# Three orders rewritten in a fused attention and SiLU kernel: v's loads ahead of the reciprocals' copies, x's sums ahead of the additions, one couple's q ahead of its k

## The chip, the cores and the metric

One core of a Trainium2 chip runs the whole kernel. Its engines are TensorE (PE, with weight loads shown apart as PEld), VectorE (DVE), ScalarE (ACT), GpSimd (POOL) and SyncE (SP), which here only issues DMAs. Each engine works through its own instructions in the order in which the program lists them, and waits on semaphores for the others. The metric is the device time of one execution in microseconds (us), taken as the median of several executions.

## The reference

`q`, `k`, `v` are 8 batches x 12 heads x 448 positions x 64 dimensions, float32. The output of attention becomes the input x of a two-layer network with 3584 tokens, 768 -> 2048 -> 768:

```python
def rmsnorm(x, g):
    rms = np.sqrt(np.mean(x * x, axis=-1, keepdims=True) + 1e-06)
    return x / rms * g
q_n, k_n = rmsnorm(q, g_q), rmsnorm(k, g_k)
scores = np.matmul(q_n, k_n.transpose(0, 1, 3, 2)) / np.sqrt(64)
attn = np.exp(scores - scores.max(-1, keepdims=True))
attn = attn / (attn.sum(-1, keepdims=True) + 1e-09)
x = np.matmul(attn, v)           # then (B,H,S,D) -> (B*S, H*D)
h = x @ w_in
out = (h / (1 + np.exp(-h))) @ w_out
```

## The kernel before, in words

**Couples.** Attention is worked off in 24 couples of four heads each, c = 0 to 23; three couples make a batch, and GROUP = 6 couples make two batches. `visit(c)` holds scores, exponentials and weighted sums of couple c, mixed with the end of couple c - 1; `between(c)` holds what lies between two visits: the transposes of the next q and k, the sums of the exponentials and their reciprocals, the rounding of `w_in` and, from c = 6 on, a share of the first layer's matmuls for the two batches finished before. From c = 12 (LATE) on, q and k come in another layout.

**The order is written by hand.** The program runs under a manual schedule, so the order in which Python calls issue instructions is the order on each engine; only different engines may overtake each other. `fill(others, prompt)` deals such work out between the first layer's matmuls.

**A couple's path.** `scores` (L712) writes a PSUM tile `sc`, of which there are two, and ACT turns it into exponentials (L717). `weigh` (L749) multiplies them with v into the two PSUM banks `av0` and `av1`. A couple's banks are read out in the next visit: by a copy (L1412) for couples 0 to 4, by the division `divide` (L808) from couple 5 on. Only then may the next couple's first `weigh` write them. `turn` (L725) writes one column of a bank by ACT or DVE, before the last `weigh` of the couple before. The last scores of a couple (LEFT) are written by ACT over a tile that the first addition `add(c, 1)` (L763, DVE) reads, so that exponential waits for this addition.

**Reciprocals and their copies.** `sum_up` adds up the exponentials on PE with ones (L783), DVE takes reciprocals in two halves (L792), and `spread` copies them over the partitions by DMA: four copies (L799), then two (L801) that wait for the four. `divide` needs them. For couples 0 and 1 the first half's reciprocal runs in the next visit (1 and 2), and the second half with `spread` at that visit's end (`inverting.pop()()`, L1446). SP issues these copies.

**v.** `load_v` (L313) loads 256 KB into the only buffer for the first two thirds of a couple's keys; it waits for the last `weigh` that reads the buffer, `weigh(c, 1, 0)` at L1447. The remaining keys have buffers of their own (L326, L329).

**q and k of the next couple.** `normalise(c)` gives four pieces, q in two halves and k in two halves. Each squares a half on ACT (L467, into one of two scratch tiles, the first halves both into one, the second halves both into the other) and reduces it on DVE (L468); then comes a tiny DVE operation (L492), POOL takes the root (L496), and for q POOL multiplies q itself (L511, two instructions). PE transposes q in `transpose_q` (L629).

**The sums of x.** The first layer is one level of Strassen's scheme with seven products (L899 in `Seven.product`, two PSUM banks `mm` in this phase). Its right-hand sides are sums of quarters of x: `right_sums` makes four DVE subtractions (L854) for each of three column blocks, `sum_x(group, 0)`, `sum_x(group, 1)`, `sum_x(group, 2)`. Block 0 needs no x of the group's last couple, blocks 1 and 2 do. They run at c = 6, 12 and 18 for the two batches before. Results are taken from the banks by DVE (L857), or by ACT (L907, L917).

**Rounding of w_in** (only at early couples): ACT L100 and L101, DVE L123, L126, L130, POOL L134; `sum_w_in` adds sums of it on DVE (L854 and L857 of 128x768).

**Late couples' q**: `sum_squares` and `scale` (L684 on PE, L685 on DVE, L688 and L691 on POOL), then `flip` (L655 on DVE).

Of the kernel before, what the change touches and what calls it, by code (L numbers as in the profile page):

```python
# [535 lines left out]
def bounded(  # L536
# [4 lines left out]
    HW, HF = z.NW // 2, z.NF // 2  # L541
# [8 lines left out]
    GROUP, LATE = z.NPAIR, z.LATE  # L550
# [88 lines left out]
    def transpose_k(c):  # L639


        assert z.KB == BANK
        t = ps.tile([P, 2, BANK], F32, name="sc", bufs=2)
        rows = place[f"k{c % 2}"]
        for i in range(2):
            for j in range(z.KEYS + 1 - i):
                nc.tensor.transpose(t[:, i, ts(j, P)], rows[:, ds((z.KA, z.KB)[i] + j * P, P)], ident)
        columns = t.rearrange("p i s -> p (i s)")[:, 0 : z.NK]
        nc.scalar.activation(kT, columns, AF.Copy, scale=gains)
        loads["k" if c < LATE - 1 else "quarters"](min(c + 2, LATE))  # L650
# [71 lines left out]
    def turn(step, copy):  # L722

        if step != weighed["step"]:
            copy(banks[1][:, S : S + 1], minus_half)  # L725
# [86 lines left out]
    def normalise(c):  # L812


        def piece(name, i):
            t = scratch[i if c < GROUP + 2 else 0]
            source = raw_of(c) if c < GROUP else q_of(c)
            if name == "q":
                norm.squares_q(c, source, t, i)
            else:  # L820
                norm.squares_k(c, place["k0" if c >= LATE else f"k{c % 2}"], t, i)
            if name == "q" and c < GROUP:
                norm.root(c, name, i)
                norm.scale(c, source, q_of(c), i, nc.gpsimd)
                if i == 1 and c + 2 < GROUP:
                    load_q(c + 2)
            elif i == 1:
                norm.root(c, name)
                if name == "q":
                    for m in range(2):  # L830
                        norm.scale(c, source, q_of(c), m, nc.gpsimd)
                elif LATE <= c < NC - 1:
                    loads["k"](c + 1)

        if c >= NC:
            return []
        return [lambda a=a: piece(*a) for a in (("q", 0), ("q", 1), ("k", 0), ("k", 1))]
# [15 lines left out]
    def minus(a, b, out):  # L853
        nc.vector.tensor_tensor(out=out, in0=a, in1=b, op=ALU.subtract)  # L854
# [11 lines left out]
                lambda: minus(a12, s2, s4),  # L866
            )[step]()

    def right_sums(b11, b12, b21, b22, t1, t2, t4):

        minus(b12, b11, t1)
        minus(b22, t1, t2)
        minus(b22, b12, b12)
        minus(b21, t2, t4)

    ps_alone = None
    turns = dict(next=0)
# [66 lines left out]
    def fetch_ahead(group, m):  # L944
        rows = [staged(), extra_stage if m else staged()]
        nc.sync.dma_start(rows[0], ahead[m])
        return rows, part_in(group, m, rows)
# [15 lines left out]
    def quarters(group, c):  # L963

        return [xT(b, c + up) for up in (0, HW) for b in group]

    def sums_of_x(c):
        return [sums_x[:, ts(i * HW + c, S)] for i in range(3)]

    def sum_x(group, c):  # L970
        right_sums(*quarters(group, c), *sums_of_x(c))

    def part_in(group, m, rows, prompt=False):

# [404 lines left out]
    def weights_in(c, half):  # L1379
        i = 2 * (c - GROUP) + half  # L1380
        work = [step_of[step] for step in halves.get(i, "ro" if c < GROUP else "")]
        return work + [lambda a=a: sum_w_in(*a) for a in sums_halves.get(i, ())]
# [8 lines left out]
    def last_two(c):  # L1391
        return [c // GROUP * 2 - 2, c // GROUP * 2 - 1]

    def visit(c):

        beside = normalise(c + 1) if 0 < c < GROUP else []
        if c < NC:
            scores(c, 0, 0)
        if c == 0:
            normalise_alone(1)  # L1400
        run_all(beside[0:1])
        if c > 0:
            weigh(c - 1, LEFT)
            weigh(c - 1, LEFT - 1, 0)
            turn(1, nc.scalar.copy if c <= GROUP else nc.vector.tensor_copy)
        if c < NC:
            scores(c, 0, 1)
        if c > 0:
            weigh(c - 1, LEFT - 1, 1)
            if c - 1 < EARLY:  # L1410
                for i in range(2):
                    nc.vector.tensor_copy(x_of(c - 1, i), sums[i])  # L1412
                run_all(beside[1:2])
                if inverting:
                    if c > 1:
                        divide(c - 2, None)
                    while len(inverting) > (c < GROUP // 2):
                        inverting.pop(0)()
            else:
                divide(c - 1, sums)  # L1420
                run_all(beside[1:2])
                if c < NC and c % GROUP == 0:
                    sum_x(last_two(c), 0)
                weights_in_visit(c)
            if c + 1 < NC:
                loads["vrest"](c + 1)
        if c == NC:
            return
        scores(c, 1, 0)
        scores(c, 1, 1)  # L1430
        if c < GROUP:
            run_all(beside[2:3])
        weigh(c, 0, 1)
        scores(c, 2, 0)
        weigh(c, 1, 1)
        turn(0, nc.scalar.copy)
        if c < GROUP:
            run_all(beside[3:4])
        scores(c, 2, 1)
        weigh(c, 0, 0)  # L1440
        run_all(add(c, 1))
        if c >= GROUP and c % GROUP == 0:
            for i in range(1, HW):
                sum_x(last_two(c), i)
        if len(inverting) == 1:
            inverting.pop()()  # L1446
        weigh(c, 1, 0)  # L1447
        if c < GROUP // 2:
            room.w_in.open()
        scores(c, LEFT)  # L1450
        if c + 1 < NC:
            loads["v"](c + 1)

    def run_all(work):
        for piece in work:
            piece()

    def between(c):

        def transposes_and_sums():  # L1460
            summing = sum_up(c)
            if c < GROUP:
                next(summing)
            if c == GROUP - 1:
                reciprocals = next(summing)
                divide(c - 1, None)
                run_all(reciprocals)
                transpose_k(c + 1)
                return
            if c < LATE - 1:  # L1470
                transpose_k(c + 1)
            reciprocals = next(summing)
            if LATE - 1 <= c < NC - 1:
                reciprocals += [lambda: flip(c + 1, "k"), gain]
            if GROUP // 2 <= c < EARLY:
                divide(c - 1, None)
            return reciprocals

        if c < LATE - 1:
            transpose_q(c + 1)  # L1480
        elif c < NC - 1:
            flip(c + 1, "q")
        if c < GROUP // 2:
            inverting.extend(transposes_and_sums())
        elif c == GROUP - 1:
            transposes_and_sums()
        if c >= GROUP and c % GROUP == 0:
            fetched = range(AHEAD) if c == GROUP else ()
            columns = products - 2 * HW * S * len(fetched)
            work = halves_in(last_two(c), range(HF), plain_in, dict(begun), fetched)  # L1490
            begin(work, columns, 2 * GROUP)
            begun.clear()
        late = add(c, LEFT - 1) + add(c, LEFT) if c >= GROUP else []
        further = normalise(c + 2) if c >= GROUP - 1 else []
        fill(late + weights_in(c, 0) + further[2:])
        prompt = transposes_and_sums() if GROUP // 2 <= c != GROUP - 1 else []
        if prompt and c < GROUP:
            prompt.insert(0, lambda: None)
        if c == GROUP // 2:
            begin(make_ahead([0, 1]), AHEAD * 2 * HW * S, GROUP - 1)  # L1500
        if c >= LATE - 2:
            if c == LATE - 2:
                prompt.append(pair_up)
            queries = prompt[3:] + [lambda: sum_squares(c + 2)]
            fill(weights_in(c, 1), prompt[:3] + [lambda: run_all(queries)])
        else:
            fill(weights_in(c, 1) + further[:2], prompt)
        if c % GROUP == GROUP - 1:
            finish()
            if c == GROUP - 1:  # L1510
                begun[0] = fetch_ahead([0, 1], 0)
        if c >= LATE - 2:
            scale(c + 2)
        if GROUP <= c < NC - 1:

            nc.scalar.activation(first, minus_half, AF.Exp)
        if c == NC - 1:
            while rounder.load():
                pass

    begun, inverting = {}, []
# [14 lines left out]
    group = [z.B - 2, z.B - 1]  # L1536
# [219 lines left out]
```

## Time and profile before

| | |
|---|---|
| median of 3 runs | 1331.36 us (1330.54, 1336.35, 1331.36) |
| profiled execution, its own time | 1330.28 us |
| its span, first to last instruction | 1328.5 us |
| PE busy | 1298.6 us, 98% of the span |
| DVE busy | 949.4 us, 71% |
| ACT / POOL busy | 505.7 us, 38% / 362.0 us, 27% |
| mean granted TensorE clock | 0.998 of full speed |

Line numbers of the form L763 are lines of the kernel before; the diff moves later lines by a few. In a timeline's rows the columns are start (us from the span's start), duration, engine, line, operation, output <- input, how many, and in brackets how long the engine had been idle and for whom it waited. In the lists of waits the numbers are us in all, how many times, and the longest.

### The profile page before, as it was taken

The numbers are of one execution on the slowest core, as the hardware profiler recorded it, in microseconds if no ns is written. First come the engines' busy times: TensorE is split into PE (matmuls) and PEld (weight loads), VectorE is DVE, ScalarE is ACT, GpSimd is POOL, SyncE is SP. The second block draws the span as 40 slices with busy tenths as digits, with TensorE's granted clock in tenths as the row PEclk, the third lists the DMA queues.
The fourth block names the chain that finished last, engine by engine and source line by source line (L and its number), as shares of the span: only waits on it lengthen the run. The fifth ranks groups of instructions, "written<-read, shape, count | busy, mean of one in ns | idle before, by whom it ended". The sixth has DMA issues, their size and how long they took to land.

```text
span 1328.5 us, 19796 instructions
## 1 busy us (share of the span) xinstructions
PE 1298.6 (98%) x7193; PEld 829.5 (62%) x7193; DVE 949.4 (71%) x1629; ACT 505.7 (38%) x886; POOL 362.0 (27%) x230
## 2 busy tenths in 40 slices
PE   8998999999999999999999999999999999999998
PEld 4343444444444444344444455558999999999998
DVE  6888777775855555754554686688978787878785
ACT  7867566645455555455545244410000000001000
POOL 6766444353234333342330144410000000000000
PEclk9999999999999999999999999999999999999999
DMA  9665337234344444344421357512323232332311
GB/s 239 163 178 139 91 90 208 80 88 95 86 116 93 97 98 113 89 94 107 95 67 46 119 174 263 166 66 76 100 76 100 77 104 82 99 107 69 128 48 39
DMA packets 249439, 144.94 MB, mean 109 GB/s; under 512 B 184292, under 2 KB 233220, under 8 KB 249332
## 3 DMA queue, kind: packets, MB, share of 16 engines
q1 hardware_dynamic: 248672, 142.42, 38.2%
q8 instruction: 59, 0.97, 0.3%
q0 software_dynamic: 352, 0.96, 0.2%
q14 instruction: 48, 0.39, 0.1%
q10 hardware_dynamic: 308, 0.20, 0.1%
HBM read 93.98 MB, written 41.29 MB: 102 GB/s over the span
## 4 chain that ended last, share of the span: by engine, by line
PE 83%; DVE 7%; ACT 4%; issue 2%; DMA 2%; POOL 1%; SPq 0%; ACTq 0%; DVEq 0%; POOLq 0%
PE mm L899 24%; PE alone L1206 22%; PE av L749 8%; PE sc L712 8%; PE mm L1206 8%; PE alone L899 7%; PE alone L1243 2%; DVE work L763 2%; PE sc L783 1%; DVE sums_x L854 1%; PE mm L1243 1%; ACT stage L1037 1%; ACT work L717 1%; DMA rows<-in_v_dram 1%; ACT L1037 1%
## 5 line engine op out<-in xcount | busy, mean ns | idle before, releaser
L899 PE MATMUL mm<-x,W 128*128 128x448 f32 x612 | 246.6, 546 | 4.6 <-DVE parts L857 2.1
L717 ACT ACTIVATE work<-sc,rms 128x448 f32<-128x448 f32 x324 | 184.7, 633 | 67.4 <-PE sc L712 62.8
L899 PE MATMUL mm<-sums_x,W 128*128 128x448 f32 x480 | 195.9, 547 | 5.5 <-DVE stage L857 3.8
L899 PEld LDWEIGHTS mm<-x,W 128*128 128x128 f32 x612 | 112.3, 190 | 131.2 <-issue 104.7
L712 PE MATMUL sc<-work 64*64 64x448 f32 x1344 | 164.3, 543 | 1.8 <-ACT work L717 1.5
L763 DVE TENSOR_TENSOR work<-work 128x896 f32<-128x896 f32 (+1 forms) x114 | 123.8, 1117 | 53.5 <-PE av L749 52.9
L749 PE MATMUL av<-work,rows 64*64 64x448 f32 x1296 | 153.4, 541 | 4.1 <-DMA rows<-in_v_dram 2.0
L899 PEld LDWEIGHTS mm<-sums_x,W 128*128 128x128 f32 x480 | 90.1, 191 | 101.0 <-issue 86.0
L496 POOL TENSOR_TENSOR rms<-rms,minus_half 128x14 f32<-128x14 f32 (+4 forms) x43 | 106.3, 2474 | 158.9 <-DVE rms L492 149.4
L523 POOL DMA_DIRECT2D out_dram<-x x2 | 1.2, 594 | 443.3 <-DVE x L857 443.3
L1206 PE MATMUL alone<-W,rows 128*128 128x192 f32 x610 | 113.0, 326 | 0.0
L749 PEld LDWEIGHTS av<-work,rows 64*64 64x64 f32 x1296 | 57.9, 132 | 75.8 <-issue 35.2
L1206 PEld LDWEIGHTS alone<-W,rows 128*128 128x128 f32 x610 | 101.5, 190 | 0.0
L712 PEld LDWEIGHTS sc<-work 64*64 64x64 f32 x1344 | 53.4, 132 | 73.0 <-ACT work L717 27.9
L919 POOL TENSOR_TENSOR parts<-parts,stage 128x448 f32<-128x448 f32 x31 | 42.0, 1356 | 148.5 <-DVE parts L857 148.1
L688 POOL TENSOR_TENSOR rms<-rms,minus_half 128x28 f32<-128x28 f32 x12 | 57.5, 4794 | 61.3 <-DVE rms L685 61.3
L1206 PE MATMUL alone<-W,work 128*128 128x192 f32 x382 | 72.2, 326 | 0.0
L1037 ACT ACTIVATE stage<-stage 128x896 f32<-128x896 f32 x63 | 57.3, 945 | 23.3 <-DVE stage L857 22.5
L468 DVE TENSOR_REDUCE rms<-rows 128x8 f32<-128x512 f32 (+2 forms) x56 | 35.8, 640 | 40.3 <-ACT rows L467 38.8
L1216 ACT COPY rows<-alone 128x192 f32<-128x192 f32 x33 | 10.5, 318 | 142.1 <-PE alone L1206 78.4
L1206 PEld LDWEIGHTS alone<-W,work 128*128 128x128 f32 x382 | 63.8, 190 | 0.0
L792 DVE RECIPROCAL work<-sc 128x224 f32<-128x224 f32 x38 | 58.6, 1546 | 5.4 <-PE sc L783 5.2
(250 smaller groups left out, 2112.6 us busy)
## 6 DMA issues: line engine op xcount, KB each, us to landing
hidden<-stage SPq DMA_DIRECT2D x63, 448.0 KB, 3.1
work<-hidden SPq DMA_DIRECT2D x21, 1024.0 KB, 5.2
rows<-in_moe_w_out_dram SPq DMA_DIRECT2D x32, 384.0 KB, 3.6
W<-in_moe_w_in_dram SPq DMA_DIRECT2D x22, 512.0 KB, 5.4
work<-work SPq DMA_DIRECT2D x141, 56.0 KB, 2.0
x<-hidden SPq DMA_DIRECT2D x7, 1024.0 KB, 5.5
rows<-in_q_dram SPq DMA_DIRECT2D x96, 56.0 KB, 2.2
rows<-in_k_dram SPq DMA_DIRECT2D x96, 56.0 KB, 2.2
```

The lines of the kernel that those rows point to most:

```text
L496: nc.gpsimd.tensor_tensor(out=t, in0=t, in1=half, op=ALU.pow)
L688: nc.gpsimd.tensor_tensor(out=f, in0=f, in1=minus_half.to_broadcast([P, n]), op=ALU.pow)
L712: nc.tensor.matmul(two[ds(half * D, D), h, 0:S], keys[rows, ts(half, D)], qT[rows, pair, :], start=True, stop=True,)
L717: nc.scalar.activation(eleft[:, h] if j == LEFT else weights(c, j)[:, i, h], two[:, h, 0:S], AF.Exp, scale=norm.column(c, i, h, j),)
L749: nc.tensor.matmul(sums[i][ds(h * D, D), :], v, w, start=(j == 0 and step == 1), stop=(j == LEFT - 1 and step == 1),)
L763: nc.vector.tensor_tensor(out=total, in0=total, in1=more, op=ALU.add)
L792: nc.vector.reciprocal(out=r[0][:, rows], in_=t[:, rows])
L899: nc.tensor.matmul(t, self.left(name, s), self.right(name, s), start=s == ends[0], stop=s == ends[1])
L919: nc.gpsimd.tensor_tensor(out=u2, in0=u2, in1=p5, op=ALU.add)
L1037: nc.scalar.activation(t, t, AF.Silu)
L1206: nc.tensor.matmul(t, x[:, i], y, start=i == ORDER[0], stop=i == ORDER[-1])
L1243: nc.tensor.matmul(o, a[:, 2 * i + m, t], right_one(name, i)[:, m], start=n == 0, stop=n == len(steps) - 1,)
```

## The change

The instructions of PE and their order are the same. Three orders differ on the other engines.

- In visits 1 and 2 `inverting.pop()()` moves from before `weigh(c, 1, 0)` to the end of the visit. DVE's order does not change by it; on SP the v load of the next couple now stands before the six copies of `spread`.
- The sums of x. For c = 6, block 0's four subtractions move to the end of `between(5)`, behind the reciprocals, and blocks 1 and 2 stand before the first additions instead of behind them. For c = 12 and 18, block 0's first two subtractions move to the end of `between(11)` and `between(17)`, ahead of L685; its last two stand behind `turn`; blocks 1 and 2 stand before the additions.
- Couple 7, the eighth: its q pieces run in `between(5)` where its k pieces ran, and the k pieces run in `visit(6)`. On POOL the root and the two multiplications of q stand ahead of the root of k and of one L134.

```diff
-    def right_sums(b11, b12, b21, b22, t1, t2, t4):
-        minus(b12, b11, t1)
-        minus(b22, t1, t2)
-        minus(b22, b12, b12)
-        minus(b21, t2, t4)
+    def right_sums(b11, b12, b21, b22, t1, t2, t4, steps=range(4)):
+        for step in steps:
+            (
+                lambda: minus(b12, b11, t1),
+                lambda: minus(b22, t1, t2),
+                lambda: minus(b22, b12, b12),
+                lambda: minus(b21, t2, t4),
+            )[step]()
...
     def visit(c):
-        beside = normalise(c + 1) if 0 < c < GROUP else []
+        beside = normalise(c + 1) if 0 < c <= GROUP else []
+        if c == GROUP:
+            beside = beside[2:]
...
             turn(1, nc.scalar.copy if c <= GROUP else nc.vector.tensor_copy)
+            if GROUP < c < NC and c % GROUP == 0:
+                sum_x(last_two(c), 0, range(2, 4))
...
                 divide(c - 1, sums)
                 run_all(beside[1:2])
                 if c < NC and c % GROUP == 0:
-                    sum_x(last_two(c), 0)
+                    for i in range(1, HW):
+                        sum_x(last_two(c), i)
...
         run_all(add(c, 1))
-        if c >= GROUP and c % GROUP == 0:
-            for i in range(1, HW):
-                sum_x(last_two(c), i)
-        if len(inverting) == 1:
-            inverting.pop()()
         weigh(c, 1, 0)
...
             loads["v"](c + 1)
+        if len(inverting) == 1:
+            inverting.pop()()
...
     def between(c):      # c == GROUP - 1, then the fills
                 run_all(reciprocals)
+                sum_x([0, 1], 0)
                 transpose_k(c + 1)
...
-        fill(late + weights_in(c, 0) + further[2:])
+        fill(late + weights_in(c, 0) + (further[2:] if c >= GROUP else further[:2]))
...
-            fill(weights_in(c, 1) + further[:2], prompt)
+            fill(weights_in(c, 1) + (further[:2] if c >= GROUP else []), prompt)
...
             if c == GROUP - 1:
                 begun[0] = fetch_ahead([0, 1], 0)
+            elif c < NC - 1:
+                sum_x([c // GROUP * 2, c // GROUP * 2 + 1], 0, range(2))
```

More of the change, by code (lines that the diff above doesn't have):

```diff
@@ L968, in sums_of_x, with sum_x @@
         return [sums_x[:, ts(i * HW + c, S)] for i in range(3)]
-    def sum_x(group, c):
-        right_sums(*quarters(group, c), *sums_of_x(c))
+    def sum_x(group, c, steps=range(4)):
+        right_sums(*quarters(group, c), *sums_of_x(c), steps)
     def part_in(group, m, rows, prompt=False):
```

## The prediction

> **What bounds the kernel now.** The page's first table says that PE is the bound, and the list of PE's own waits, with its stretches, says what is left to win.
>
> ```profile
> PE 1298.6 (98%) x7193; PEld 829.5 (62%) x7193; DVE 949.4 (71%) x1629; ACT 505.7 (38%) x886; POOL 362.0 (27%) x230
> ```
>
> PE is not busy for 1328.5 - 1298.6 = 29.9 us. Since the change leaves PE's instructions alone, it can only move these 29.9 us, or the clock. The waits of PE (matmuls) over the whole run, then those of 110 to 134 us:
>
> ```profile
> PE mm L899 <- DVE stage L857: 5.4, 4, 1.9
> PE av L749 <- DMA rows<-in_v_dram: 3.1, 2, 2.0
> PE sc L629 <- POOL x L511: 2.5, 2, 1.7
> ...
> PE mm L899 <- DVE sums_x L854: 0.6, 1, 0.6
> ```
>
> ```profile
> PE av L749 <- ACT av L725: 1.3, 1, 1.3
> ```
>
> Each sits where the change works: v in visits 2 and 3; L725, L511 and sums_x in visit 6 and just behind it; and of the four L857 waits two, 1.91 and 1.88 us, in couples 12 and 18. Timelines of the three places:
>
> ```profile
> 40.87 3.82 SPq L801 DMA_DIRECT2D work<-work  x2
> 44.78 0.54 SPq L313 DMA_DIRECT2D rows<-in_v_dram  x1
> 64.29 1.15 DVE L808 TENSOR_TENSOR x<-x,work 128x448 f32<-128x448 f32 x2
> 64.33 0.98 PE L749 MATMUL av<-x,rows 64*64 64x448 f32 x8 [1.11 <-DMA rows<-in_v_dram]
> 70.63 1.16 ACT L717 ACTIVATE work<-sc,rms 128x448 f32<-128x448 f32 x2 [1.77 <-DVE x L763]
> ```
>
> ```profile
> 119.11 0.63 ACT L467 ACTIVATE rows<-x 112x512 f32<-112x512 f32 x1 [0.45 <-DVE rms L468]
> 123.12 1.16 DVE L808 TENSOR_TENSOR x<-av,work 128x448 f32<-128x448 f32 x2
> 126.69 3.33 POOL L496 TENSOR_TENSOR rms<-rms,minus_half 112x16 f32<-112x16 f32 x1
> 131.63 0.60 PE L629 MATMUL sc<-ident,x 112*128 112x112 f32 x4 [1.71 <-POOL x L511]
> ```
>
> ```profile
> 332.10 1.16 DVE L808 TENSOR_TENSOR x<-av,work 128x448 f32<-128x448 f32 x2 [1.32 <-PE av L749]
> 333.82 2.07 DVE L854 TENSOR_TENSOR sums_x<-x,sums_x 128x448 f32<-128x448 f32 x1
> 338.35 2.09 DVE L763 TENSOR_TENSOR work<-work 128x896 f32<-128x896 f32 x2 [1.38 <-PE av L749]
> 347.88 0.62 DVE L857 TENSOR_TENSOR stage<-mm,stage 128x448 f32<-128x448 f32 x1
> 348.55 2.52 PE L899 MATMUL mm<-sums_x,W 128*128 128x448 f32 x6 [1.91 <-DVE stage L857]
> ```
>
> In the last, DVE idles 1.32 and 1.38 us and then makes PE wait 1.91 us behind its own backlog. Couple 18 repeats it; there the granted clock (the column of 1.00, 0.97, 0.50) falls afterwards:
>
> ```profile
> 551.00:553.00 2.00, 1.83 (x5) 0.57 (x3) 2.00 (x3) 0.00 (x0) 0.00 (x0) 1.00 0.00 0
> 553.00:555.00 2.00, 0.29 (x1) 0.29 (x2) 2.00 (x4) 0.00 (x0) 0.00 (x0) 0.97 0.59 97
> 555.00:557.00 2.00, 2.00 (x4) 0.78 (x4) 1.97 (x3) 0.00 (x0) 0.00 (x0) 0.50 0.70 112
> ```
>
> **Part 1, v ahead of spread.** Visit 1's v load (for couple 2) is issued at 44.78 because SP stands at the second L801, which waits for the L799 copies. Its own condition, `weigh(1, 1, 0)`, is met at 35.3, and SP is done with L329 at 36.5. So it goes out at 36.5; even the longest landing of the early v loads, 7.0 us, is 43.5, before PE needs v (45.8). The six copies behind it lose nothing in issue, as their reciprocal ends at 38.2. PE's 2.03 us go; late next is ACT: four L717 to 47.40, one L467 (0.65), two L717, then L725 at 49.1 instead of 50.70. PE gains 1.6. In visit 2 the load for couple 3 goes at 53.8 instead of 61.36 and PE's 1.11 us go too, but visit 3 ends on DVE: it is packed from 60.6 to 73, L808 at 64.29 leads over two L792 to L763 at 69.43, ACT's L717 waits for that (1.77) and PE's L647 for ACT. So PE keeps what L808 gains. L808 needs couple 1's copies, which landed at about 62.6 (L801 issued by 61.3, landing 1.9 from issue start). The DMA engines are full there (share 1.00, 268 GB/s at 51 to 53), so 256 KB ahead of the copies cost 1.0 us: L808 at 63.6, gain 0.7; if the queue absorbs them, 1.6. I take **-1.0**. Ends: -3.1 (both waits); +0.8, if v lands only after 7.8 us like L326 of that stretch and L808 comes at 65.1.
>
> **Part 2, couple 6.** First DVE's ledger from the reciprocals' end (116.15) to L808 (123.12), without a gap before. Added in it: four subtractions of 0.62, 2.5. Taken out: the second k reduction and its L492, 0.7. POOL's L134 stays at 121.6, behind L801, and then meets the L492 of q, at 122.2: +0.8, as L126 took 1.42 beside an L134 (at 57.4) instead of 0.43. L808 itself reads PSUM and stayed at 611 to 625 ns in all 38 instances, so POOL does not hold it. It comes at 125.7, **2.6 late**, and PE's first `weigh` of couple 6, which needs the banks, at 126.4 instead of 123.80. ACT's side is covered by that: k's first square needs the scratch that q's reduction frees at 121.6, so L725 comes at 122.4 instead of 121.20, and PE idles 2.4 instead of 1.3 us there, but both end before the banks are free.
>
> What comes back: POOL runs q's L496 and L511 from 123 to 128 (before 126.69 to 132.95), and PE reaches L629 at 132.5, so 1.71 + 0.78 go. Blocks 1 and 2 are done by 134.4 even when they wait for an L511 and an L134, before the second run of sums_x matmuls, so 0.62 goes. Net 2.6 - 2.5 - 0.6 = **-0.5**. The additions follow at 134.4 (before 128.58); ACT's last L717 waits for them till 135.5, but ACT's next result that PE needs is L917 at 139. Rounding's first three steps come 2.5 later on DVE, its second L134 behind L511, k's root later: couple 7's exponentials use it at 157. SP's L942 store waits for L857, some 3 us later; what follows on SP (the fetch L946, L326, L329) is used at 137 and after. Ends: -1.3 (L492 slips ahead of L134); +3.8 (2.6 more if L496 also blocks DVE, and 1.7 for a clock drop).
>
> [...]
>
> **Part 3, couples 12 and 18.** Block 0's first two subtractions (1.25) go in before L685 (328.59), which ends at 330.1; the scores that need its PSUM tile come at 330.32, and L725 waits for PE till 330.62 anyway. The last two fill 330.8 to 332.0, where DVE idles 1.32 before L808. So L808 stays at 332.1. Blocks 1 and 2 follow from 333.2: eight by 0.62 is 5.0, plus 1.5 for one stop beside L691 (the 2.07 row), now 1.25 later: done at 339.8. L763 comes at 339.8 instead of 338.35; ACT's last L717 must wait for the first of them, till 340.9 (before 339.77), and ends at 342.1, just when L907 (342.17) needs ACT. Then L655 to 343.0, two L763 to 345.0, and L857 at 345.0 instead of 347.88, while PE reaches the wait at 346.6. The 1.91 goes whole; next late is PE itself. Couple 18 the same: -1.88, and the clock drop with it: the six sums_x matmuls took 4.22 there, 2.52 in couple 12, so -1.7. **-1.9 and -3.6.** Ends: 0, if ACT's L717 makes L907 late; -5.5.
>
> [...] Here 1.88 idle was followed by 0.50, and 1.91 at 348 and 2.03 at 47 were not. [...]
>
> **Sum.** -1.0 - 0.5 - 1.9 - 3.6 = -7.0, so 1323.3 against the profiled execution's 1330.28, which is 1.1 under the median; against the median of 1331.36, **1324.4 us**. A measurement tells about 0.5% (6.7 us) from no change; this is at that edge.
>
> **Rivals.**
> - *The early orders only swap waits*: the copies land late (+0.8) and DVE's longer ledger costs couple 6 +2.1. With -5.5 from couples 12 and 18: -2.6, **1328.8**. For it, DMA share 1.00 around 50 us and DVE without a gap at 116 to 123; against, L808's slack of 1.6 at 64.3.
> - *ACT takes L857's place in couples 12 and 18*: additions behind eight subtractions hold L717, then L907, then the mm bank. It starts at 0.1 + 1.5 us more delay than I count (L907 ends 342.7, the bank is wanted at 344.2) and eats 1.9 at 3.5. Then -1.5, **1329.9**. Against: only one stop beside L691 is possible.
> - *All waits go whole*: -3.1 - 1.3 - 1.9 - 3.6 = -9.9, **1321.5**.
> - *Slower*: PE's clock in couple 6. PE idles there 2.4 and 1.2 us within 6 us; if this, as in couple 18, gives 0.50 and PE stays too thin to leave it until 133.45, its work there (13.3 us from 120.15, less 3.8 idle: 9.5) takes twice as long, +9.5 - 7.0 = +2.5, **1333.9**. It decides from 7.0 us of work at half clock. Against: 1.3, 1.7 and 0.8 idle in that place cost no clock before.
>
> **How the numbers follow.** Chances: forecast 0.51, swapped waits 0.20, ACT 0.10, all gone 0.14, clock 0.05. The forecast's own band is 1322.5 to 1327.5, and some two thirds of it lie over 0.5% below; with all gone, faster 0.47. Slower by over 0.5% (1338) needs the clock drop and a second loss: 0.04. Within: 0.49. The range runs from -9.9 on the profiled time (1320.4) to no change (1331.4), which leaves out the clock rival and half of the tails.
>
> **What would show it.** L313 of visits 1 and 2 at about 36.5 and 53.8 and no PE wait on in_v; L808 of visit 3 at 62.5 to 64; L808 of visit 6 some 9 us after the reciprocals instead of 7; no PE wait on L511; no PE wait on L857 in couples 12 and 18 and clock 1.00 there. Wrong if PE waits longer for av banks in visit 6 than 4 us in all, if L907 in couples 12 and 18 waits for ACT instead of PE, or if half clock appears in visit 6.

## The result and the profile after

The changed kernel takes **1323.76 us** (median of 8 executions, 1323.12 to 1328.70); the kernel before, run beside it, takes 1332.03 us (median of 8, 1329.52 to 1336.35). The ratio is 0.9943, 95% interval 0.9926 to 0.9959: 0.57% faster, with an interval that includes the 0.5% that was called the edge of what can be told. The prediction was 1324.4 us. The profiled execution took 1323.70 us, its span 1321.9 us, against 1330.28 and 1328.5 before.

The first table of the page and the first rows of PE's own waits over the whole run, of the kernel after (engine, tile and line that waited <- what it waited for: us in all, times, longest):

```profile
PE 1298.3 (98%) x7193; PEld 829.3 (63%) x7193; DVE 949.2 (72%) x1629; ACT 505.2 (38%) x886; POOL 361.5 (27%) x230
```

```profile
PE mm L902 <- DVE parts L857: 3.6, 7, 1.2
PE av L749 <- ACT av L725: 2.2, 2, 2.0
PE sc L647 <- ACT work L717: 2.0, 1, 2.0
PE mm L902 <- DVE stage L857: 1.6, 2, 0.9
```

The busy time of all engines is the same to 0.5 us; what PE stands idle falls from 29.9 to 1321.9 - 1298.3 = 23.6 us. L902, L910 and L712 of this kernel are L899, L907 and L712 of before; L808, L763, L857 keep their numbers. The waits on `in_v` (3.1) are out of the list, the wait on POOL's L511 over `x` (2.5) and that on `sums_x` (0.6) are too, and `stage` L857 falls from 5.4 to 1.6. New or larger are L647's wait for ACT's L717 (2.0), that for L725 (2.2 instead of 1.5), that for `parts` L857 (3.6 instead of 3.0) and that for the copy out of the banks (0.7 instead of 0.2).

Where the time went is seen best from the moment at which PE starts each visit. The table gives how much PE gains (negative) or loses between one such moment and the next one shown, against before, worked out from the starts of the first scores in PE's timeline (the first row counts from the span's start, the last one to its end), for the change and for those experiments that do one part alone:

| PE, from the start of visit ... to ... | after | v only | sums of 12, 18 only | couple 6 only | its q first only | its sums only |
|---|---|---|---|---|---|---|
| start to 3 | -1.86 | -1.83 | +1.27 | +1.34 | +0.01 | +0.10 |
| 3 to 6 | +1.41 | +1.20 | +0.09 | +2.59 | -0.07 | +0.13 |
| 6 to 7 | -0.64 | +0.31 | +0.01 | -0.50 | +2.95 | -0.56 |
| 7 to 12 | +0.26 | +0.10 | +0.09 | +0.79 | +0.56 | +0.79 |
| 12 to 13 | -2.17 | 0.01 | -2.17 | 0.01 | 0.01 | 0.00 |
| 13 to 18 | -0.01 | -0.02 | 0.00 | -0.02 | -0.02 | -0.02 |
| 18 to 19 | -3.83 | 0.00 | -3.83 | 0.01 | 0.00 | 0.00 |
| 19 to 23 | +0.01 | 0.00 | +0.01 | 0.00 | +0.01 | +0.01 |
| 23 to end | +0.24 | +0.57 | +0.03 | +0.05 | +0.31 | +0.38 |

The +1.27 and +1.34 of the first row, and the +2.59 of the second, are drops of TensorE's clock at places which those two kernels do not touch (the +2.59 together with a longer wait for v, 2.87 instead of 1.11 us); they are taken up at the end. So is the clock drop in the +2.95. The last row lies behind every changed instruction, so differences of some tenths of a us between two executions tell nothing.

**Visits 1 to 4 (part 1)**, timeline of after. Columns as before: start, duration, engine and line, and in brackets how long the engine had been idle and for whom:

```profile
36.80 0.54 SPq L313 DMA_DIRECT2D rows<-in_v_dram  x1
...
53.52 0.54 SPq L313 DMA_DIRECT2D rows<-in_v_dram  x1
...
60.76 1.14 SPq L801 DMA_DIRECT2D work<-work  x2
63.40 1.16 DVE L808 TENSOR_TENSOR x<-x,work 128x448 f32<-128x448 f32 x2 [0.89 <-DMA work<-work]
69.76 1.16 ACT L717 ACTIVATE work<-sc,rms 128x448 f32<-128x448 f32 x2 [3.69 <-DVE x L763]
70.97 0.98 PE L647 MATMUL sc<-ident,rows 128*128 128x128 f32 x7 [2.05 <-ACT work L717]
75.24 1.16 DVE L808 TENSOR_TENSOR x<-x,work 128x448 f32<-128x448 f32 x2 [2.19 <-DMA work<-work]
```

v leaves 8 us earlier (36.80 instead of 44.78) and nobody waits for it. But in visit 3 the division L808, at 63.40 instead of 64.29, now itself waits 0.89 us for the copies; L763 waits for the division, ACT's L717 for L763 (3.69) and PE's L647 for L717 (2.05). PE's gain there is what L808 gained: 71.84 became 70.97. One visit later the next L808, which waits for its copies in both kernels, comes at 75.24 instead of 75.69, and 0.45 us are left of 1.86. The row of before:

```profile
75.69 1.16 DVE L808 TENSOR_TENSOR x<-x,work 128x448 f32<-128x448 f32 x2 [1.77 <-DMA work<-work]
```

The 0.45 is the reading of one execution. The variant with two early subtractions (below) has the same instructions as after up to couple 5, and in its execution the copies landed 0.38 us later:

```profile
63.78 2.02 DVE L808 TENSOR_TENSOR x<-x,work 128x448 f32<-128x448 f32 x2 [1.29 <-DMA work<-work]
...
72.21 1.76 PE L647 MATMUL sc<-ident,rows 128*128 128x128 f32 x7 [3.31 <-ACT work L717]
```

The second half of L808, which reads SBUF here, then ran beside POOL's L511 (at 64.28) and took 1.48 us instead of 0.62; PE stood 3.31 us instead of 2.05, the clock fell behind that (0.53 in the window from 72 to 74 us), and PE started visit 6 1.33 us later than before instead of 0.45 earlier. Whether part 1 gains or loses is thus not settled by one profile.

**Couple 6 (part 2)**, timeline and windows of after. A window's row gives its length, then busy time (and number of instructions) of PE, PEld, DVE, ACT and POOL, the granted clock, the DMA share and GB/s:

```profile
121.48 1.30 POOL L134 TENSOR_TENSOR W<-W 128x512 int32<-128x512 int32 x1
121.52 1.31 DVE L492 TENSOR_SCALAR rms<-rms 112x16 f32<-112x16 f32 x1
121.67 1.73 PE L749 MATMUL av<-work,rows 64*64 64x448 f32 x8 [1.97 <-ACT av L725]
122.91 3.04 POOL L496 TENSOR_TENSOR rms<-rms,minus_half 112x16 f32<-112x16 f32 x1
123.16 2.69 PE L712 MATMUL sc<-work 64*64 64x448 f32 x16
123.19 0.43 DVE L126 TENSOR_SCALAR W<-W 128x512 int32<-128x512 int32 x1
...
125.39 1.15 DVE L808 TENSOR_TENSOR x<-av,work 128x448 f32<-128x448 f32 x2
126.02 2.04 POOL L511 TENSOR_TENSOR x<-x,rms 112x512 f32<-112x512 f32 x2
126.06 1.12 PE L749 MATMUL av<-work,rows 64*64 64x448 f32 x6 [0.21 <-DVE x L808]
...
132.11 0.99 PE L629 MATMUL sc<-ident,x 112*128 112x112 f32 x8
132.93 1.31 PE L902 MATMUL mm<-sums_x,W 128*128 128x448 f32 x3
```

```profile
118.36:121.77 3.41, 1.44 (x20) 0.41 (x16) 3.34 (x6) 1.88 (x5) 0.78 (x2) 1.00 0.08 21
121.77:125.18 3.41, 3.41 (x20) 1.20 (x24) 3.34 (x6) 1.50 (x4) 3.29 (x2) 0.50 0.56 129
```

L808 comes 2.3 us later than before (2.7, since PE started the visit 0.45 earlier) and with it the first `weigh` of the couple (126.06 instead of 123.80). What comes back: the eight transposes L629 go in one run, with no wait for L511, and the sums are ready when PE asks for them. After the 1.97 us wait the clock is at 0.50, and 16 matmuls take 2.69 us; but PE would have waited for L808 until 126.0 in any case, as the 0.21 says.

**Couple 12 (part 3)**, timeline of after; couple 18 behaves alike, and there the clock stays up (a window, second fence):

```profile
331.27 1.16 DVE L808 TENSOR_TENSOR x<-av,work 128x448 f32<-128x448 f32 x2 [0.26 <-PE av L749]
338.37 2.09 DVE L763 TENSOR_TENSOR work<-work 128x896 f32<-128x896 f32 x2
339.55 1.16 ACT L717 ACTIVATE work<-sc,rms 128x448 f32<-128x448 f32 x2 [1.82 <-DVE work L763]
341.34 0.53 ACT L910 COPY stage<-mm 128x448 f32<-128x448 f32 x1 [0.63 <-PE mm L902]
343.40 4.67 PE L902 MATMUL mm<-sums_x,W 128*128 128x448 f32 x12
343.67 0.62 DVE L857 TENSOR_TENSOR stage<-mm,stage 128x448 f32<-128x448 f32 x1 [0.22 <-PE mm L902]
```

```profile
549.00:551.00 2.00, 2.00 (x7) 1.06 (x6) 1.40 (x3) 0.00 (x0) 0.00 (x0) 1.00 0.64 106
```

DVE's idle 1.32 ahead of L808 has shrunk to 0.26. L857 now waits for PE, not PE for L857, and the twelve `sums_x` matmuls, which were cut by a wait of 1.91 us after the first half, go in one run.

### The profile page after: what moved, and what is told of

The parts are those of the page before. It is cut to its first block, busy times and chain, and to the rows that moved or that the text cites. A ratio compares the mean times of both kernels' runs of the same rounds, so it can differ in the third digit from the quotient of the medians.

```text
span 1321.9 us, 19806 instructions
## 1 busy us (share of the span) xinstructions
PE 1298.3 (98%) x7193; PEld 829.3 (63%) x7193; DVE 949.2 (72%) x1629; ACT 505.2 (38%) x886; POOL 361.5 (27%) x230
## 4 chain that ended last, share of the span: by engine, by line
PE 83%; DVE 6%; ACT 4%; DMA 3%; issue 2%; POOL 1%; SPq 1%; ACTq 0%; DVEq 0%; POOLq 0%
PE mm L902 25%; PE alone L1209 23%; PE mm L1209 8%; PE av L749 8%; PE sc L712 7%; PE alone L902 7%; PE alone L1246 2%; PE sc L783 1%; DMA work<-work 1%; DVE work L763 1%; DVE work L792 1%; ACT work L717 1%; PE mm L1246 1%; ACT stage L1040 1%; DMA hidden<-stage 1%
## 5 line engine op out<-in xcount | busy, mean ns | idle before, releaser
L902 PE MATMUL mm<-x,W 128*128 128x448 f32 x612 | 246.7, 546 | 4.7 <-DVE parts L857 2.0
L717 ACT ACTIVATE work<-sc,rms 128x448 f32<-128x448 f32 x324 | 184.8, 634 | 71.9 <-PE sc L712 58.0
L902 PE MATMUL mm<-sums_x,W 128*128 128x448 f32 x480 | 193.4, 543 | 1.5 <-DVE parts L857 1.5
L902 PEld LDWEIGHTS mm<-x,W 128*128 128x128 f32 x612 | 112.3, 190 | 131.1 <-issue 104.3
L712 PE MATMUL sc<-work 64*64 64x448 f32 x1344 | 165.6, 546 | 1.8 <-ACT work L717 1.5
L763 DVE TENSOR_TENSOR work<-work 128x896 f32<-128x896 f32 (+1 forms) x114 | 123.7, 1118 | 50.1 <-PE av L749 49.6
L749 PE MATMUL av<-work,rows 64*64 64x448 f32 x1296 | 154.1, 543 | 3.3 <-ACT av L725 2.2
L902 PEld LDWEIGHTS mm<-sums_x,W 128*128 128x128 f32 x480 | 89.6, 190 | 95.2 <-issue 85.5
L496 POOL TENSOR_TENSOR rms<-rms,minus_half 128x14 f32<-128x14 f32 (+4 forms) x43 | 105.2, 2449 | 149.2 <-DVE rms L492 139.6
L749 PEld LDWEIGHTS av<-work,rows 64*64 64x64 f32 x1296 | 57.8, 132 | 75.7 <-issue 35.8
L712 PEld LDWEIGHTS sc<-work 64*64 64x64 f32 x1344 | 53.6, 133 | 74.8 <-ACT work L717 29.2
L1040 ACT ACTIVATE stage<-stage 128x896 f32<-128x896 f32 x63 | 57.3, 945 | 23.6 <-DVE stage L857 22.9
```

The source lines that it names most:

```text
L496: nc.gpsimd.tensor_tensor(out=t, in0=t, in1=half, op=ALU.pow)
L712: nc.tensor.matmul(two[ds(half * D, D), h, 0:S], keys[rows, ts(half, D)], qT[rows, pair, :], start=True, stop=True,)
L717: nc.scalar.activation(eleft[:, h] if j == LEFT else weights(c, j)[:, i, h], two[:, h, 0:S], AF.Exp, scale=norm.column(c, i, h, j),)
L749: nc.tensor.matmul(sums[i][ds(h * D, D), :], v, w, start=(j == 0 and step == 1), stop=(j == LEFT - 1 and step == 1),)
L763: nc.vector.tensor_tensor(out=total, in0=total, in1=more, op=ALU.add)
L902: nc.tensor.matmul(t, self.left(name, s), self.right(name, s), start=s == ends[0], stop=s == ends[1])
```

## The experiments

No experiment leaves out any of the work. "Before" below is the kernel before, run beside them on the same chip: 1332.68 us for the first four, 1332.8 us for the last four (medians).

### One part alone: v

```diff
-        if len(inverting) == 1:
-            inverting.pop()()
         weigh(c, 1, 0)
...
             loads["v"](c + 1)
+        if len(inverting) == 1:
+            inverting.pop()()
```

> The kernel before with the first part alone: v's load ahead of spread in visits 1 and 2. Theory (DVE's chain through the copies keeps most of it): both PE waits on in_v are gone, PE is 1.9 us ahead at the start of visit 3, 0.9 at the start of visit 4 and 0.45 at the start of visit 5; span -0.4 to -0.6 us. Rival (the waits are the price): all 3.1 us stay to the end. Rival (queued copies): no gain or a loss by visit 5, and the 0.45 seen in the changed kernel came from elsewhere.

Measured: 1331.89 us (1329.66 to 1333.94), ratio 0.9992 (0.9980 to 1.0004). PE's waits from 30 to 134 us in this kernel:

```profile
PE sc L629 <- POOL x L511: 2.5, 2, 1.7
PE sc L647 <- DMA work<-work: 1.8, 1, 1.8
PE av L749 <- ACT av L725: 1.3, 1, 1.3
```

`in_v` is gone from it and L647 has taken its place, in the same visit as in after; the table's 1.83 us shrink to 0.63 by visit 6 and to 0.22 by visit 23, and its whole span is 0.4 us longer than that of before (1328.9 against 1328.5). The chain through the copies, L808, L763 and L717 thus belongs to this part, without the other two. The rival that both v waits (3.1 us) go whole falls.

### One part alone: the sums of couples 12 and 18

```diff
             turn(1, nc.scalar.copy if c <= GROUP else nc.vector.tensor_copy)
+            if GROUP < c < NC and c % GROUP == 0:
+                sum_x(last_two(c), 0, range(2, 4))
...
-                if c < NC and c % GROUP == 0:
+                if c == GROUP:
                     sum_x(last_two(c), 0)
+                elif c < NC and c % GROUP == 0:
+                    for i in range(1, HW):
+                        sum_x(last_two(c), i)
...
-        if c >= GROUP and c % GROUP == 0:
+        if c == GROUP:
...
+            elif c < NC - 1:
+                sum_x([c // GROUP * 2, c // GROUP * 2 + 1], 0, range(2))
```

`right_sums` and `sum_x` take `steps` as in the change.

> The kernel before with the x sums of couples 12 and 18 alone moved; couple 6 as before. Theory: PE's waits on L857 in couples 12 and 18 (1.91 and 1.88 us) are gone and so is the half clock behind the second, so the profiled span is 5.5 to 6.2 us shorter, and most of the whole change's 8 us of median is here; the runs lie closer together than those of the kernel before, since clock drops behind these two gaps come and go. Rival (ACT takes their place): span 0 to -2 us, with a wait on L907. Rival (the scatter has another source): the same span, but runs spread over 5 us or more as before.

Measured: 1325.78 us (1325.17 to 1328.67), ratio 0.9951 (0.9934 to 0.9967): 6.9 of the 8.3 us by which after is faster. The steps in the table are those of after, -2.17 and -3.83, to the hundredth, and no ACT wait takes the place of the one removed: the rival with ACT falls. The profiled span is 4.5 us shorter and not the 5.5 to 6.2 expected: a clock drop at 10 us took 1.25 of the 6.0. Five of six executions lie within 1.5 us.

### One part alone: couple 6 whole

```diff
-        beside = normalise(c + 1) if 0 < c < GROUP else []
+        beside = normalise(c + 1) if 0 < c <= GROUP else []
+        if c == GROUP:
+            beside = beside[2:]
...
-                if c < NC and c % GROUP == 0:
+                if c == GROUP:
+                    for i in range(1, HW):
+                        sum_x(last_two(c), i)
+                elif c < NC and c % GROUP == 0:
                     sum_x(last_two(c), 0)
...
-        if c >= GROUP and c % GROUP == 0:
+        if c > GROUP and c % GROUP == 0:
...
                 run_all(reciprocals)
+                sum_x([0, 1], 0)
...
-        fill(late + weights_in(c, 0) + further[2:])
+        fill(late + weights_in(c, 0) + (further[2:] if c >= GROUP else further[:2]))
...
-            fill(weights_in(c, 1) + further[:2], prompt)
+            fill(weights_in(c, 1) + (further[:2] if c >= GROUP else []), prompt)
```

> The kernel before with couple 6's part alone: block 0 of the x sums behind the reciprocals, blocks 1 and 2 ahead of the additions, and couple 7's q ahead of its k. Theory: L808 comes some 2.3 us later, the waits on L511 and sums_x (3.1 us) go, PE is 0.5 to 0.7 us ahead at the start of visit 7, span -0.3 to -0.7. Rival (clock): the longer gap before L725 gives half clock that is not covered by the wait for the banks, span +1 or more. Rival (all of it): -1.3 or better.

Measured: 1331.94 us (1328.88 to 1335.23), ratio 0.9990 (0.9978 to 1.0002). Visit 6 gains 0.50 us, as forecast, although the clock fell in it too; visits 7 to 12 give 0.79 back (PE's wait for L857 in visit 8 grows from 0.95 to 1.73 us). The profiled execution is 4 us over that of before because of drops at 10 and 68 us; the windows show the second of these and the one in visit 6:

```profile
68.00:70.00 2.00, 2.00 (x19) 0.91 (x15) 2.00 (x3) 0.00 (x0) 0.86 (x1) 0.53 0.82 209
...
126.00:128.00 2.00, 1.95 (x12) 0.79 (x16) 1.97 (x3) 1.49 (x3) 1.88 (x2) 0.54 0.68 159
```

The three parts alone bring 0.8, 6.9 and 0.7 us in medians, 8.4 together, and after brings 8.3, which fits parts that add up. But the 0.8 and the 0.7 by themselves cannot be told from nothing, so only the 6.9 is shown.

### Couple 6 cut in two: q first alone, and the sums alone

The first takes only the three edits of `beside` and of the two fills shown above (the couple's q ahead of its k). The second takes only the other edits, those of the sums.

> The kernel before with only couple 7's q pieces ahead of its k pieces; the x sums stay in the old order. Theory (the sums ahead of L808 are what costs, q first is what earns): L808 0.5 to 1 us earlier, no wait on L511 (2.5 us), but the sums of blocks 0 to 2 and the additions still stand in the old order, so PE's wait on sums_x grows from 0.6 to about 2.5 us and eats most of it: span -0.3 to -1.2. Rival (q first is worth its whole wait): -2.5. Rival (q first is worth nothing without the sums): 0.

> The kernel before with only couple 6's x sums moved (block 0 behind the reciprocals, blocks 1 and 2 ahead of the additions); couple 7's k pieces stay ahead of its q. Theory (the two orders of couple 6 pay only together): L808 comes some 2.5 us later, and q's chain on POOL too, so PE waits for L511 about as long as before or longer; visit 7 starts 0.5 to 2.5 us later than before, more with a clock drop. Rival (the sums alone earn the 0.5 us of couple 6): visit 7 starts 0.5 us earlier.

Measured: q first alone 1335.32 us (1330.54 to 1338.64), ratio 1.0020 (1.0006 to 1.0034), slower; the sums alone 1333.10 us (1330.08 to 1335.18), ratio 1.0003 (0.9991 to 1.0015). With q first alone, the wait for POOL's L511 over `x` goes, and PE comes to the sums 2.4 us earlier than before (131.01 against 133.45) and stands there. Waits from 110 to 148 us, timeline and windows of that kernel:

```profile
PE mm L899 <- DVE sums_x L854: 3.1, 2, 1.8
```

```profile
133.77 1.02 PE L899 MATMUL mm<-sums_x,W 128*128 128x448 f32 x2 [1.82 <-DVE sums_x L854]
...
136.03 6.31 PE L899 MATMUL mm<-sums_x,W 128*128 128x448 f32 x8 [1.24 <-DVE sums_x L854]
```

```profile
136.00:138.00 2.00, 1.97 (x3) 1.15 (x4) 2.00 (x4) 0.00 (x0) 0.00 (x0) 0.50 0.00 0
...
140.00:142.00 2.00, 2.00 (x4) 0.93 (x3) 1.94 (x3) 0.00 (x0) 0.00 (x0) 0.50 0.00 0
```

Then the clock falls to 0.50 and eight matmuls take 6.31 us instead of 3.27. These 3.0 us are the whole loss of visit 6 (2.95): apart from the clock, q first alone gains nothing there. It is the kind of loss that the prediction's slower rival gave for couple 6, at a later place, and it came with half of the edit. My expectation of a gain from q alone was wrong: L808 came 0.35 us later and not earlier, as it had to wait 0.97 for its copies, and I had priced the wait on `sums_x` at 2.5 and not the clock behind it.

With the sums alone, PE comes later to L629 (133.60), because it stands 3.54 us before L725 and 1.15 for L808, so L511 is ready without q's change; visit 6 gains 0.56, as much as with both (0.64 and 0.50). My claim that the two orders pay only together is not borne out by visit 6. Neither pays in the median.

### Trying to get the lost part back

Two variants of the changed kernel, and both together: v's load between the four copies and the two, so that the copies of couple 1 go first in the queue; and at couple 6 only the first two subtractions of block 0 ahead of L808, the rest behind.

```diff
+            while between_copies:
+                between_copies.pop()()
...
-        if c + 1 < NC:
-            loads["v"](c + 1)
         if len(inverting) == 1:
+            between_copies.append(lambda: loads["v"](c + 1))
             inverting.pop()()
+        elif c + 1 < NC:
+            loads["v"](c + 1)
```

(the first two lines stand in `spread`, between the four copies and the two)

```diff
-                        sum_x(last_two(c), i)
+                        sum_x(last_two(c), i, range(2) if c == GROUP else range(4))
+                    for i in range(HW if c == GROUP else 0):
+                        sum_x(last_two(c), i, range(2, 4))
...
-                sum_x([0, 1], 0)
+                sum_x([0, 1], 0, range(2))
```

> The changed kernel, with v's load of visits 1 and 2 issued between spread's four copies and its two instead of ahead of all six. Theory (v's 256 KB in the full DMA queue hold up the four copies): the copies of visit 2 land about 1 us earlier, L808 of visit 3 comes at 62.4 to 62.8 instead of 63.40, visit 4 starts 0.6 to 1 us earlier than in the changed kernel; L808 of visit 4 is held by copies behind w_in loads, so by visit 5 0 to 0.6 is left. Rival (v was not in the way of the copies): L808 unchanged at 63.4. Rival (v comes too late now): a wait on in_v in visit 2 or 3.

> The changed kernel, with only the first two of block 0's subtractions ahead of the rounding in couple 6; the other two, and the last two of blocks 1 and 2, follow behind the first two of blocks 1 and 2. Theory (the ledger of DVE ahead of L808 sets visit 6): L808 comes 1.2 us earlier (124.2 instead of 125.4), L725 too, the gap before L725 shrinks from 2.0 to about 0.8 us and its half clock goes, and PE starts its sums_x matmuls 1.2 us earlier: -1.0 to -1.3 us against the changed kernel. Rival (something else holds L808 or the sums come late): 0 or slower.

> The changed kernel with v between the copies and the two early subtractions together. Theory: the sum of the two, -1.0 to -1.9 us against the changed kernel, and the fastest of all; the runs as close together as the changed kernel's. Rival: the first does not last beyond visit 5, so the time is that of the second alone.

Measured: 1324.33 us (1323.33 to 1326.08), ratio 0.9934 (0.9918 to 0.9951); 1325.04 us (1323.30 to 1327.05), 0.9938 (0.9921 to 0.9954); 1324.79 us (1323.30 to 1327.23), 0.9936 (0.9920 to 0.9953). None is told apart from after.

In the first (its L804, L811 and L750 are L801, L808 and L749), v for couple 3 leaves at 60.24 instead of 53.52 and the two copies are no earlier. Timeline:

```profile
60.24 0.38 SPq L313 DMA_DIRECT2D rows<-in_v_dram  x1
...
62.48 1.15 SPq L804 DMA_DIRECT2D work<-work  x2
63.29 0.98 PE L750 MATMUL av<-x,rows 64*64 64x448 f32 x8 [0.68 <-DMA rows<-in_v_dram]
...
65.13 2.01 DVE L811 TENSOR_TENSOR x<-x,work 128x448 f32<-128x448 f32 x2 [1.38 <-DMA work<-work]
```

A clock drop at 10 us has put this execution 1.25 us back, so the division at 65.13 is 0.5 us later than after's 63.40, not 1 us earlier, and so are the copies. PE waits for v again, 0.68 us: the rival that v comes too late was right. The execution of both variants together had no drop before this place and says the same: its division comes at 64.17, and PE waits 1.02 us for v. My reason, that v's 256 KB ahead of the copies hold them up, falls in this form: the position in the queue was changed and the landing was not advanced. What sets the copies' landing is not settled.

In the second, L808 of couple 6 does come 0.9 us earlier, once the 1.8 us are taken off by which this execution was behind after at the start of visit 6, and the half clock is not seen there; the wait for L725 shrinks to 0.90 us. But PE then waits 2.04 us for L808 (after 0.21), and L857 has moved behind the other sums and three L763, and PE waits for it. Timeline:

```profile
126.25 1.14 DVE L808 TENSOR_TENSOR x<-av,work 128x448 f32<-128x448 f32 x2
...
139.39 0.61 DVE L857 TENSOR_TENSOR parts<-mm,stage 128x448 f32<-128x448 f32 x1
140.06 2.15 PE L902 MATMUL mm<-x,W 128*128 128x448 f32 x5 [1.59 <-DVE parts L857]
```

So visit 6 to 7 loses 0.42 where after gains 0.64. In both variants together the clock fell in this visit, at 128 us, behind a wait of 2.24 us for L808. DVE has no room in couple 6: what one wait gets back the next one takes.

## Why the prediction was right, and where it was not

**The sum.** Predicted -7.0 on the profiled time; measured 1330.28 - 1323.70 = 6.6. On the medians -8.3, and 1323.76 us lies 0.6 us under the forecast. That it lies so near is in part luck: in the profile parts 1 and 3 miss by about half a us each in opposite directions, and 0.26 and 0.24 us are given back in visits 7 to 12 and behind visit 23, which the sum does not have. The difference of 1.7 between the two comes from the kernel before: its profiled execution is 1.75 us under its median of 1332.03, and that of after lies on its own. Before scatters over 6.8 us, after, but for one execution, over 1.5. The mean granted clock goes with it: over the 42 executions of before, those at 0.998 average 1330.4 us, at 0.997 1332.1, at 0.996 1333.4 and at 0.993 1336.7; seven of the eight of after stand at 0.998 or 0.999 with 1323.1 to 1324.6, and the eighth, 1328.7, at 0.994. Part of what the median gains is thus probably fewer clock drops per execution. That is a correlation over executions without a profile; which drops they had is not known. In the profiled ones the drop behind couple 18 is in all five with the old order there (before and four experiments) and in none of the five with the new one.

**Part 1, -1.0: the mechanism was right, the size was not.** v left at 36.8 and 53.5 (forecast 36.5, 53.8), L808 came at 63.4 (63.6), and PE got 0.87 of its 1.86 at visit 4, where L808 led over L763 and L717 to L647 as written. The mis-sized step is "PE keeps what L808 gains": it was followed for one visit only. In the next one L808 waits for the copies of couple 2, which landed only 0.45 sooner, and that is what PE kept. It measured -0.45 by visit 6, and -0.22 by visit 23 where the part stands alone; another execution with the same instructions had +1.33 by visit 6, and the median of the part alone cannot be told from before.

**Part 2, -0.5: right in the net, -0.64.** L808 and the first `weigh` were 2.7 late relative to the start of the visit (forecast 2.6). The four subtractions added 2.2 (forecast 2.5), L492 beside L134 took 1.31 (the forecast added 0.8 to its 0.17), L511 ran to 128.1 (128), the transposes and the sums came without a wait: 2.7 - 2.5 - 0.6, and 0.26 more because the twelve `sums_x` matmuls run uncut (4.69 us instead of 1.68 + 3.27). I had named half clock in visit 6 as a sign against the forecast, and it appeared, at 0.50. The rival decides from 7.0 us of work at half clock; here it was 2.7 (0.98 and 1.68 us of weighing and scores at full clock, as in the kernel with the sums alone, 1.73 and 2.69 here), and it lay in front of the wait for L808: that kernel waits 1.15 for L808 where after waits 0.21. So the sign of being wrong appeared and cost nothing; naming it had been too strict. Not foreseen: visits 7 to 12 give 0.26 back, with the couple alone 0.79. It is seen in visit 8, where PE's wait for L857 grows from 0.95 to 1.17 (alone 1.73) behind an ACT copy that waits for the store of `hidden`.

**Part 3, -1.9 and -3.6: right, -2.17 and -3.83.** L808 kept its place relative to PE; L763 came 0.85 later (338.37 with after 0.83 ahead) and not 1.45; L857 waits for PE; the drop at couple 18 left with its gap. ACT's L717 had to wait for L763 as forecast (1.82 us idle, till 339.55) and L910 followed at 341.34 only 0.63 after ACT became free, when PE had finished. Couples 12 and 18 gained 0.26 us each beyond the wait and the drop: the cut itself had cost that, as two sixes of `sums_x` matmuls took 2.42 + 2.52 us and the twelve in one run 4.67.

**What the rows decided.** The drop at 555 us left with its gap of 1.88 us, as the sum had it. The length of one gap does not decide in this case: 1.97 us idle at 121.67 was followed by 0.50, and in the kernel with the sums alone 3.54 us in the same place by 1.00 (the last section compares them). Its timeline and windows:

```profile
123.91 0.98 PE L749 MATMUL av<-work,rows 64*64 64x448 f32 x8 [3.54 <-ACT av L725]
```

```profile
121.00:123.00 2.00, 0.00 (x0) 0.00 (x0) 1.97 (x4) 1.40 (x3) 1.80 (x2) 1.00 0.41 100
123.00:125.00 2.00, 1.09 (x12) 0.52 (x16) 1.93 (x5) 1.94 (x5) 1.97 (x1) 1.00 0.51 116
```

The +3.8 among the ends of part 2 and the +2.1 of the rival with the swapped waits hold 2.6 us for q's L496 on POOL holding up DVE. In couple 6 no run shows that term. Beside q's L496, from 122.91 to 125.95, DVE's L126 at 123.19 took 0.43 us, as it did at 120.11 in before with POOL idle (1.42 beside an L134, at 57.42), and the rounding ran from 122.75 on; L808 was 2.3 late, and visit 6 gained 0.64.

**The rivals.** The early orders that only swap waits: this is what happened to half of part 1, to q first alone and to the variant with two subtractions, but not to couples 12 and 18, which carry the result. ACT in L857's place: fell. All waits whole: fell at L647. Slower by half clock in couple 6: with the whole change the half clock came, lasted 3.41 us (121.77 to 125.18) where the rival had it last until 133.45, and was covered by the wait for L808; a loss by it was seen with q first alone (+2.95 in visit 6), behind the sums.

## What to carry to other kernels

A wait at which one engine idles first and then makes another wait behind its own backlog (DVE's 1.32 and 1.38 us ahead of L857) is real money: filling the idle with the backlog's work brought 6.9 of the 8.3 us, -6.0 us from step to step where the rows had said -5.5. Before counting a removed wait, find the next one in the same stage and follow the gain through the visit after; q first alone removed 2.5 us of waits, met 3.1 us of others and a clock drop, and came out 0.2% slower. A part worth half a us cannot be read from one execution: 0.38 us in the landing of a copy, with L808 beside L511 and a clock drop behind it, became 1.8 us two visits later. A median can gain more than a profile (here 8.3 us against 6.6), perhaps because the change takes away a gap such as that of 1.88 us in couple 18, behind which the clock fell to 0.50 in before.

## What the runs showed that I had not expected

The granted clock fell to half at different places in different executions: at 10 us in three (a window of the kernel with the sums of couples 12 and 18 alone, below; after had 1.00 there, with the same instructions), at 68 to 74 in three, at 122 to 128 in three, at 135 with q first alone and, in the five with the old order in couple 18, at 555 to 560.

```profile
10.00:12.00 2.00, 2.00 (x16) 0.81 (x18) 1.54 (x3) 0.00 (x0) 1.82 (x2) 0.56 1.19 195
```

One drop cost PE 1.25 us (at 10 us) to 1.7 (at 555); the longest, with q first alone, cost 3.0.

Several followed a gap of about 2 us, but gaps of 1.91 us (at 348.55 in before) and 3.54 us (the sums alone) did not bring one, so the length of the gap alone does not decide. Each of these drops lasts 3.41 us (121.77 to 125.18 in after, 554.87 to 558.28 in before; the one at 135 us twice that, 6.83). From the end of its one drop to the half clock behind PE's last work, before has 768.0 us (to 1326.29) and after 1194.7 us (to 1319.85), 225.0 and 350.0 times 3.413. The variant with v between the copies can be laid beside after, because it has after's instructions in couple 6 and the same gap of 1.97 us ahead of L725 (L726 there). Its timeline, and two windows of 3.41 us, counted off from its drop at 10 us:

```profile
123.67 0.98 PE L750 MATMUL av<-work,rows 64*64 64x448 f32 x8 [1.97 <-ACT av L726]
```

```profile
119.47:122.88 3.41, 2.23 (x24) 0.61 (x16) 3.34 (x7) 1.90 (x4) 0.40 (x1) 1.00 0.19 50
122.88:126.29 3.41, 2.49 (x24) 0.82 (x24) 3.31 (x7) 2.92 (x7) 3.27 (x3) 1.00 0.50 118
```

In after, counted off from its drop in the same way, the whole gap lies in one such window, in which PE is busy 1.44 of 3.41 us, and the next window shows 0.50 (the windows under couple 6). Here a window ends inside the gap, PE is busy 2.23 and 2.49 us, and the clock stays at 1.00. PE then waits 1.42 us for L808, which again shows that after's half clock was covered; that visit 6 gains 1.13 here and not 0.64 lies with DVE, whose L492 took 0.82 us beside L134 instead of 1.31. The gap of 3.54 us was divided in the same way, between windows with 1.79 and 1.50 us busy. Counted off like this over the ten profiled executions, their ends left out, 14 windows had PE busy for at most 0.45 of the time, and 12 of them were followed by a drop (1.44 us busy in after; 1.53 in before, from 551.46). The two others had 0.44 (the 1.50 us above) and 0.45 (1.52 us, in before from 346.66). Of all other windows only three were followed by one, all at about 7 us and with 0.54 to 0.59. These are counts in the traces of this case; no experiment changed PE's busy time in a window by itself, and what sets off a drop, what is different at 7 us and why one drop lasted 6.83 us is not shown.

The profiled executions of three of the eight experiments were set back by a drop before the first changed instruction, which is why their parts are read here from the steps between visits and not from the spans.
